# Softmax reciprocals as powers of minus one on GpSimd, in an attention and feed-forward kernel

## The chip, the cores and the metric

The kernel runs on one core of a Trainium2 chip. The core has five engines with an instruction queue each: TensorE (PE in the profile; its weight loads are listed apart as PEld), VectorE (DVE), ScalarE (ACT), GpSimd (POOL) and SyncE (SP), which here only issues transfers. An engine works through its queue strictly in order; semaphores make an instruction wait for one of another engine, or of its own. The metric is the device time of one execution in microseconds (us).

## What is computed

```
def _attn_ref(q, k, v):                      # (8, 8, 576, 64) each
    scores = scale * np.matmul(q, k.transpose(0, 1, 3, 2))
    kth = np.partition(scores, -32, axis=-1)[..., -32:-31]
    scores = np.where(scores >= kth, scores, -1000000000.0)
    scores = scores - np.max(scores, axis=-1, keepdims=True)
    attn = np.exp(scores)
    attn = attn / (np.sum(attn, axis=-1, keepdims=True) + 1e-09)
    return np.matmul(attn, v)

def _moe_ref(x, w_in, w_out):                # 4608 rows, 512 -> 2048 -> 512
    r = np.maximum(x @ w_in, 0.0)
    return (r * r) @ w_out
```

Attention over 8 batches of 8 heads keeps, for each query, only the 32 largest of its 576 scores. Its result, heads side by side, goes through a feed-forward layer with a squared relu.

## The kernel before

**Tiles.** Heads are taken in pairs (32 pairs), and the queries of a pair in blocks of 128 (four, and a rest of 64 that is joined with the rest of the next pair). That makes 144 groups; each group holds two heads' scores of 128 queries, 2 x 576 columns.

**One group.** PE makes the scores in PSUM, and ScalarE copies them to the tile `s` (L651). VectorE folds them with maxima into a tile `f` (L715, three folds). GpSimd does integer arithmetic on the same tiles (L710): two instructions write `u`, and one writes the low half of `f` from `u` and `f`; this last one is called "low" in this text. VectorE then finds the 32nd largest score by rounds of eight maxima and match-replace (L736, L741, L745, L748; result `kth`). ScalarE makes a mask `w` (L756), PE transposes scores and adds the mask (L476, L473), and ScalarE takes the exponential, `p` (L804). PE multiplies with V, to which a column of ones has been added, so that column 64 of each 65 holds the softmax sum.

**Where the change is.** This is the function `collect`: ScalarE copies the product from PSUM to `av` (L833), VectorE takes the reciprocals of column 64 into `rzall` (L835), GpSimd multiplies by them and writes `x` in bf16 (L837), and SP issues a transposing transfer of `x` into `xt` (L847, L850). `collect` is called 88 times: 56 times for two groups together (4 columns of `rzall`), 32 times for one (2 columns). `rzall` is read once more at the end, where `verdict` checks its largest and smallest element (L1027, L1028).

**The feed-forward part** (`feed`) takes `xt` in chunks: PE multiplies with the first weights, ScalarE applies the relu (L879), the square is taken by GpSimd (L893), ScalarE (L896) or, for the last two chunks, VectorE (L890); PE multiplies with the second weights, ScalarE copies (L913), and SP stores (L921).

**The order.** Nothing in the code says in which order an engine works. Each operation is entered with its engine, an assumed duration, a priority (lower goes first) and its dependencies; `late` delays the moment from which it may be taken. A planner (`Plan.schedule`) plays this through and, whenever an engine is free, takes the ready operation with the lowest priority. The five orders so found are emitted, with the semaphore waits that the dependencies need. Priorities are times: `tg` is a group's due time, `tt` the one at which its attention product is due. Buffers are given out in the same play; `f` has four, `u` one, `av` three, `x` four.

A second plan follows in the program, a full search that runs only when `verdict` raises a flag.

Of the kernel before, what the change touches and what calls it, by code (L numbers as in the profile page):

```python
# [5 lines left out]
ALU = mybir.AluOpType  # L6
# [6 lines left out]
P = 128  # L13
# [296 lines left out]
def bass_top_k_attn__then__act_relu_squared_kernel(  # L310
# [24 lines left out]
    def sb(name, shape, dt=FP32, n=None):  # L335
        if n is None:
            return nc.alloc_sbuf_tensor(name, shape, dt)
        return [nc.alloc_sbuf_tensor(f"{name}{i}", shape, dt) for i in range(n)]
# [27 lines left out]
    LATE = 2.3  # L366
# [14 lines left out]
    rzall = sb("rzall", [P, NALL])  # L381
    fcmp = sb("fcmp", [P, NALL])
    fone = sb("fone", [P, 4])
    heads = sb("heads", [P, 2])
    flag = sb("flag", [1, 1], I32)
    win = sb("win", [P, NCT, DFF], BF16)
# [27 lines left out]
    def tile(nm):  # L414
        return Tile(pools[nm])

    def at(t):
        return mem[t.pool.name][t.slot]

    def bank(t, i=0):  # L420
        return ps32[:, BASE[t.pool.name] + t.slot + i, :]
# [9 lines left out]
    act, vec, gp, pe = nc.scalar, nc.vector, nc.gpsimd, nc.tensor  # L431
# [40 lines left out]
    def mm(o, l, r, start, stop=True):  # L472
        return pe.matmul(o, l, r, start=start, stop=stop, skip_group_check=True)  # L473
# [6 lines left out]
    def build(full, weights, pl):  # L480
# [331 lines left out]
        def collect(gi, groups, parts, hp, tt):  # L812

            av, avs, xr = Tile(psum), tile("av"), tile("x")
            nu = 2 * len(groups)
            r0 = state["u"]
            state["u"] += nu

            def fav(j, pt, vbs):
                o, pq = bank(av), at(pt)  # L820
                for h in range(2):
                    for qs, vb in ((slice(0, 64), vbs[0]), (slice(64, 128), vbs[-1])) if gi == Z else ((slice(0, 128), vbs[h]),):
                        vv, ou = at(vb), o[qs, 65 * (2 * j + h):65 * (2 * j + h) + 65]
                        for kb in range(4):
                            mm(ou, pq[:, 4 * h + kb, qs], vv[:, 4 * h + kb, :], j == 0 and h == 0 and kb == 0)
                        ins = mm(ou, pq[:, 8, qs], vv[:, 8 + h, :], False)
                return ins

            pts = [pt for pt, _ in groups]
            vbu = sorted({v for _, vbs in groups for v in vbs}, key=lambda t: t.num)  # L830
            pl.op("pe", .05 + .16 * nu, tt + 2, lambda: [fav(j, pt, vbs) for j, (pt, vbs) in enumerate(groups)][-1],
                  r=pts + vbu, w=[av], take=[av, avs, xr])
            pl.op("act", .19 + 65 * nu / 1200, tt + 3, lambda: act.copy(  # L833
                at(avs)[:, 0:nu, :], bank(av)[:, 0:65 * nu].rearrange("p (u c) -> p u c", c=65)), r=[av], w=[avs])
            rz = pl.op("dve", .1, tt + 4, lambda: vec.reciprocal(rzall[:, r0:r0 + nu], at(avs)[:, 0:nu, 64]), r=[avs], late=LATE)  # L835
            rzs.append(rz)
            pl.op("gp", .13 + .11 * nu, tt + 4, lambda: gp.tensor_tensor(  # L837
                at(xr)[:, 0:nu, :], at(avs)[:, 0:nu, 0:64],
                rzall[:, r0:r0 + nu].unsqueeze(2).broadcast_to([P, nu, 64]), ALU.mult),
                r=[avs], w=[xr], after=[rz])  # L840

            xt, col, first = parts

            def turn():
                x = at(xr)
                if gi == Z:
                    return [nc.sync.dma_start_transpose(  # L847
                        at(xt)[:, hp + i, col:col + 64].unsqueeze(1),
                        x[64 * i:64 * i + 64, 0:2, :].rearrange("p h d -> p (h d)")) for i in range(2)]
                return [nc.sync.dma_start_transpose(  # L850
                    at(xt)[:, hp, col:col + 64 * nu].rearrange("p (i q) -> p i q", q=P),
                    x[:, 0:nu, :].rearrange("p h d -> p (h d)"))]

            nd = 2 if gi == Z else 1
            pl.op("sp", 2.0, tt + 5, turn, r=[xr], w=[xt], take=[xt] if first else [], ndma=nd, bw=.5 * nd,
                  sem=lambda o: f"x{xr.slot}")
# [80 lines left out]
        for b in range(NB):  # L937
# [3 lines left out]
            for hp, gi in seq:  # L941
# [8 lines left out]
                tt = tg + PER + 2 - TA - TL * max(0, 1 - (NGRP - state["n"]) / NL)  # L950
# [5 lines left out]
                r0, n_ = 128 * js[0], 128 * len(js) if gi != Z else 64  # L956
# [12 lines left out]
    def setup(pl):  # L969
        i0 = pl.op("gp", .2, -100, lambda: gp.memset(ident32[:, :], 0.0))  # L970
        i1 = pl.op("gp", .3, -99, lambda: gp.affine_select(
            ident32[:, :], ident32[:, :], [[-1, P]], ALU.not_equal, 1.0, base=0, channel_multiplier=1), after=[i0])
        i2 = pl.op("gp", .3, -98, lambda: gp.tensor_copy(ident_bf[:, :], ident32[:, :]), after=[i1])
        i3 = pl.op("gp", .5, -97, lambda: gp.tensor_scalar(
            neg_bf[:, :], ident32[:, :], -1.0, None, ALU.mult), after=[i1])
        i4 = pl.op("gp", .5, -97, lambda: gp.tensor_scalar(
            steep_bf[:, :], ident32[:, :], STEEP, None, ALU.mult), after=[i1])
        h0 = pl.op("gp", .1, -97, lambda: gp.memset(heads[:, :], 0.0))
        h1 = pl.op("gp", .1, -96.9, lambda: gp.memset(heads[0:64, 0:1], 1.0), after=[h0, i2, i3, i4])
        h2 = pl.op("gp", .1, -96.8, lambda: gp.memset(heads[64:128, 1:2], 1.0), after=[h1])  # L980
        pre = [i2, i3, i4]
        for t in mem["vb"]:
            pre.append(pl.op("gp", .2, -96.5, lambda t=t: gp.memset(t[:, 0:8, D:D + 1], 1.0), after=[h2]))
            pre.append(pl.op("gp", .2, -96.4, lambda t=t: gp.tensor_copy(t[:, 8:10, D], heads[:, :]), after=[h2]))
        zeros = [pl.op("gp", .3, -97.5, lambda t=t: gp.memset(t[:, 8:10, :], 0.0)) for t in mem["rv"]]
        pre.append(pl.op("gp", .1, -95, lambda: gp.memset(fone[:, 3:4], 1.0)))
        weights = []
        wi = moe_w_in.rearrange("(ct p) f -> p ct f", p=P)
        wo_ap = moe_w_out.rearrange("(fb p) o -> p fb o", p=P)
        for i in range(16):  # L990
            s = tile("ws")
            if i < 8:
                half, ct = divmod(i, NCT)
                src = wi[:, ct, 1024 * half:1024 * half + 1024]
                dst = win[:, ct, 1024 * half:1024 * half + 1024]
                view = lambda s: at(s)[:, :]
            else:
                fb = 2 * (i - 8)
                src = wo_ap[:, fb:fb + 2, :]
                dst = wo[:, fb:fb + 2, :]  # L1000
                view = lambda s: at(s)[:, :].rearrange("p (f o) -> p f o", f=2)
            pl.op("sp", 4.0, WD * i - 60, lambda s=s, src=src, view=view: [nc.sync.dma_start(view(s), src)],
                  w=[s], take=[s], ndma=1, sem=lambda o: f"ws{o.takes[0].slot}", nbf=WN + WP * i, bw=BW * 2.5)
            eng, fn = ("act", act.copy) if i % 4 < WA else ("gp", gp.tensor_copy)
            weights.append(pl.op(eng, 1.1, WC * i, lambda s=s, dst=dst, view=view, fn=fn: fn(dst, view(s)), r=[s]))

        times = [.22 * i for i in range(int(WARM / .22))]
        times += [WARM + WSTEP * i for i in range(int((WEND - WARM) / WSTEP))]
        for x in times:
            t = Tile(psum)  # L1010
            pl.op("pe", .22, 1e5, lambda t=t: mm(bank(t), ident_bf[:, :], ident_bf[:, :].unsqueeze(1).broadcast_to(
                [P, 4, P]), True), w=[t], take=[t], after=[i2], nbf=x)
        return [i1], pre, zeros, weights
# [22 lines left out]

    main = Plan()
    early, pre, zeros, weights = setup(main)
    n_pre = len(main.ops)
    kths, rzs = build(False, weights, main)  # L1040
# [84 lines left out]
```

## Time and profile before

| what | us |
|---|---|
| median of 3 runs | 816.22 (814.95 to 816.54) |
| profiled execution | 815.42 |
| its span | 813.6 |
| VectorE busy | 773.0 |
| ScalarE busy | 704.8 |
| GpSimd busy | 701.0 |
| PE busy | 712.3 |
| 88 reciprocals on VectorE, sum of their durations | 14.1 |
| 88 multiplications on GpSimd | 46.9 |

The span runs from the first instruction that the profile shows to the last, the profiled execution's time has what lies around it as well. Busy time counts overlapping instructions of an engine once, while the sum of a group's durations counts them in full. A group's row reads: line, engine, operation, written tile <- read tiles, shapes, count | busy us, mean ns of one | idle time of the engine just before them and who ended it. A row of the waits reads: who waited <- for whom: us in total, times, longest.

### The profile page before, as it was taken

How to read it: one execution, taken by the hardware profiler on the slowest of the kernel's cores; microseconds unless marked ns; L12 is line 12 of the kernel's file. 1: busy time of each engine (PE TensorE's matmuls, PEld its weight loads, DVE VectorE, ACT ScalarE, POOL GpSimd, SP SyncE). 2: the span in 40 equal slices, each digit the busy share in tenths (PEclk: the TensorE clock that was granted, in tenths of full speed). 3: DMA queues.
4: the chain of work that ended last, by engine and by line, in shares of the span. 5: the costliest groups of instructions: out<-in, count | busy, mean ns of one | idle time of the engine just before them, and what ended most of it. 6: DMA issues, size and time to landing. Idle time of an engine off the chain costs nothing.

```text
span 813.6 us, 27365 instructions
## 1 busy us (share of the span) xinstructions
PE 712.3 (88%) x10399; PEld 531.1 (65%) x10457; DVE 773.0 (95%) x3711; ACT 704.8 (87%) x1057; POOL 701.0 (86%) x645
## 2 busy tenths in 40 slices
PE   8886888988889989888888989898798989999995
PEld 3564666666676666766677666666667666676773
DVE  3899999999999999999999999999999999999991
ACT  3888989999898898988989899999989889998881
POOL 6798998899999898998889887998889978999940
PEclk9999999999999999999999999999999999999999
DMA  8557342031320232211430123302232020100111
GB/s 194 128 155 193 103 114 60 13 85 39 92 65 13 67 77 72 52 35 34 97 92 7 36 65 93 81 18 53 50 90 54 9 61 7 50 11 20 37 34 34
DMA packets 146205, 52.74 MB, mean 65 GB/s; under 512 B 138384, under 2 KB 138384, under 8 KB 146064
## 3 DMA queue, kind: packets, MB, share of 16 engines
q1 hardware_dynamic: 145392, 50.73, 25.1%
q8 instruction: 84, 1.38, 0.7%
q14 instruction: 57, 0.47, 0.2%
q10 hardware_dynamic: 672, 0.16, 0.1%
HBM read 36.70 MB, written 9.44 MB: 57 GB/s over the span
## 4 chain that ended last, share of the span: by engine, by line
DVE 61%; PE 18%; ACT 16%; issue 3%; POOL 1%; DMA 0%; SPq 0%; DVEq 0%; POOLq 0%
DVE f L745 17%; PE ps L473 15%; DVE f L715 15%; DVE c L741 13%; DVE f L736 8%; DVE kth L748 7%; ACT s L651 5%; ACT p L804 4%; ACT w L756 3%; PE ps L476 3%; ACT g L879 2%; ACT g L896 1%; ACT av L833 1%; DVE rzall L835 0%; POOL g L893 0%
## 5 line engine op out<-in xcount | busy, mean ns | idle before, releaser
L710 POOL TENSOR_TENSOR f<-u,f 128x864 int32<-128x864 int32 x144 | 269.6, 1872 | 6.4
L745 DVE MATCH_REPLACE8 f<-c,f 128x98 f32<-128x98 f32 (+2 forms) x864 | 228.1, 271 | 0.0
L756 ACT ACTIVATE w<-s,kth 128x576 bf16<-128x576 f32 x288 | 215.4, 783 | 7.4 <-DVE kth L748 6.9
L710 POOL TENSOR_TENSOR u<-f,s 128x576 int32<-128x576 int32 x144 | 188.2, 1307 | 30.9 <-DVE f L715 30.3
L473 PE MATMUL ps<-qk 64*128 64x192 f32 (+3 forms) x1280 | 192.1, 435 | 25.0 <-DVE f L715 24.1
L741 DVE MAX8 c<-f 128x8 f32<-128x98 f32 (+2 forms) x864 | 211.1, 275 | 0.0
L651 ACT COPY s<-ps 128x1152 f32<-128x1152 f32 x144 | 161.2, 1120 | 52.0 <-PE ps L473 51.2
L804 ACT ACTIVATE p<-ps 128x1152 bf16<-128x1152 f32 x144 | 163.3, 1134 | 18.1 <-PE ps L473 17.3
L473 PEld LDWEIGHTS ps<-qk 64*128 64x128 f32 (+1 forms) x1280 | 131.3, 177 | 65.2 <-DVE f L715 40.2
L473 PE MATMUL ps<-xt,win 128*128 128x256 bf16 (+1 forms) x1152 | 130.0, 266 | 14.4 <-ACT av L833 4.6
L710 POOL TENSOR_TENSOR u<-s 128x288 int32<-128x288 int32 x144 | 114.7, 796 | 30.5 <-ACT s L651 23.1
L476 PEld LDWEIGHTS ps<-ident,s 64*128 64x128 f32 x2592 | 107.9, 141 | 42.1 <-ACT w L756 28.8
L473 PE MATMUL ps<-wo,g 128*128 128x512 bf16 x518 | 122.8, 379 | 9.0 <-issue 5.1
L715 DVE TENSOR_TENSOR f<-ps,f 128x288 f32<-128x288 f32 x288 | 127.4, 442 | 0.2
L476 PE MATMUL ps<-ident,s 64*128 64x64 f32 x2592 | 110.5, 228 | 17.3 <-ACT w L756 17.2
L473 PEld LDWEIGHTS ps<-xt,win 128*128 128x128 bf16 x1152 | 98.5, 100 | 34.3 <-ACT g L879 6.5
L748 DVE MAX8 kth<-f 128x8 f32<-128x296 f32 x288 | 120.4, 457 | 0.0
L736 DVE MAX8 f<-f 128x8 f32<-128x288 f32 x288 | 119.0, 449 | 0.0
L879 ACT ACTIVATE g<-ps 128x512 bf16<-128x512 f32 x144 | 84.3, 604 | 10.0 <-PE ps L473 10.0
L473 PEld LDWEIGHTS ps<-wo,g 128*128 128x128 bf16 x576 | 51.4, 98 | 57.8 <-ACT av L833 1.3
L715 DVE TENSOR_TENSOR f<-ps,s 128x288 f32<-128x288 f32 x144 | 65.5, 455 | 16.7 <-ACT s L651 13.5
L473 PE MATMUL ps<-vb,p 128*128 128x65 bf16 (+1 forms) x1600 | 63.4, 197 | 13.6 <-ACT qk L602 4.2
(63 smaller groups left out, 741.4 us busy)
## 6 DMA issues: line engine op xcount, KB each, us to landing
rv<-in_v_dram SPq DMA_DIRECT2D x64, 128.0 KB, 2.5
out_dram<-o SPq DMA_DIRECT2D x32, 256.0 KB, 2.1
rk<-in_k_dram SPq DMA_DIRECT2D x63, 128.0 KB, 2.5
rq<-in_q_dram SPq DMA_DIRECT2D x62, 128.0 KB, 2.5
g<-in_moe_w_in_dram SPq DMA_DIRECT2D x8, 512.0 KB, 4.0
g<-in_moe_w_out_dram SPq DMA_DIRECT2D x8, 512.0 KB, 3.6
xt<-x SPq DMA_TRANSPOSE x72, 2.4
rq<-in_q_dram SPq DMA_DIRECT2D x32, 32.0 KB, 2.5
```

The source lines that it names most:

```text
L473: return pe.matmul(o, l, r, start=start, stop=stop, skip_group_check=True)
L476: return pe.matmul(o, i, ident, is_transpose=True, skip_group_check=True, **kw)
L651: cp = [pl.op("act", 1.2, tg - LEAD + 1, lambda: act.copy(at(st)[:, :, 0:S], two(banks(ss)[:, FIRST_AT:], SECOND, S)), r=[ss], w=[st])]
L710: return pl.op("gp", dur, prio, lambda: gp.tensor_tensor(o().bitcast(I32), x().bitcast(I32), y().bitcast(I32), op), **kw)
L715: return dve(.36, lambda: vec.tensor_tensor(o(), two(banks(ss)[:, FIRST_AT + c:], SECOND, QUART), x(), ALU.max), r=[ss], **kw)
L736: prev[i] = [dve(.065 + HALF / 960, lambda i=i: vec.max(at(f)[:, i, A + 7:A - 1:-1], at(f)[:, i, M + QUART:E]), after=prev[i] + [low], hol ...
L741: lambda i=i, t=t, c0=c0, c1=c1: vec.max(eighth(t, i), at(f)[:, i, c0:c1]),
L745: lambda i=i, t=t, c0=c0, c1=c1: vec.match_replace(at(f)[:, i, c0:c1], eighth(t, i), at(f)[:, i, c0:c1], NEG), hold=[f])]
L748: ks.append(chain(kth, i, prev[i], .065 + (8 + HALF) / 960, lambda i=i: vec.max(eighth(kth, i), at(f)[:, i, A:M + QUART]), hold=[f]))
L756: masks[i:] = [pl.op("act", .77, tw + .8 * i, lambda i=i: act.activation(at(wt)[:, i, :], at(st)[:, i, 0:S], ACTF.Relu, bias=kth[:, i, n:n ...
L804: return act.activation(at(pt)[:, :, :].rearrange("p c (h q) -> p h c q", h=2), bass.AP(x.tensor, x.offset, [x.ap[0], [APART, 2], [64, 9], ...
L879: return act.activation(at(g)[:, 0:kf * nt], bank(hh)[:, 0:kf * nt], ACTF.Relu)
```

## The change

The reciprocal is no longer taken by VectorE. GpSimd raises the sum to the power -1, with a constant tile `inv` of minus ones as the second operand, and its priority is 0.1 lower than that of the multiplication which follows. The assumed duration is the same 0.1 us; the delay `late=LATE` (2.3 us) is gone. The setup has one memset more, for `inv`.

```
@@ -832,7 +833,8 @@
             pl.op("act", .19 + 65 * nu / 1200, tt + 3, lambda: act.copy(
                 at(avs)[:, 0:nu, :], bank(av)[:, 0:65 * nu].rearrange("p (u c) -> p u c", c=65)), r=[av], w=[avs])
-            rz = pl.op("dve", .1, tt + 4, lambda: vec.reciprocal(rzall[:, r0:r0 + nu], at(avs)[:, 0:nu, 64]), r=[avs], late=LATE)
+            rz = pl.op("gp", .1, tt + 3.9, lambda: gp.tensor_tensor(
+                rzall[:, r0:r0 + nu], at(avs)[:, 0:nu, 64], inv[:, 0:nu], ALU.pow), r=[avs])
             rzs.append(rz)
@@ -976,9 +978,10 @@
         h0 = pl.op("gp", .1, -97, lambda: gp.memset(heads[:, :], 0.0))
-        h1 = pl.op("gp", .1, -96.9, lambda: gp.memset(heads[0:64, 0:1], 1.0), after=[h0, i2, i3, i4])
+        i5 = pl.op("gp", .1, -97, lambda: gp.memset(inv[:, :], -1.0))
+        h1 = pl.op("gp", .1, -96.9, lambda: gp.memset(heads[0:64, 0:1], 1.0), after=[h0, i2, i3, i4, i5])
-        pre = [i2, i3, i4]
+        pre = [i2, i3, i4, i5]
```

Both plans are built from the same functions, and the planner lays out all five engines' orders anew. In the new order each power waits for ScalarE's copy; between a power and its multiplication stands mostly one other instruction of GpSimd.

More of the change, by code (lines that the diff above doesn't have):

```diff
@@ L383, in bass_top_k_attn__then__act_relu_squared_kernel @@
     fone = sb("fone", [P, 4])
+    inv = sb("inv", [P, 4])
     heads = sb("heads", [P, 2])
```

## The prediction

> **What bounds the kernel now.** I read the page first (engine shares, chain), then who VectorE waited for, then busy time by stage, then the timeline around single reciprocals, and last the chain's final part.
>
> ```profile
> span 813.6 us, 27365 instructions
> PE 712.3 (88%) x10399; PEld 531.1 (65%) x10457; DVE 773.0 (95%) x3711; ACT 704.8 (87%) x1057; POOL 701.0 (86%) x645
> DVE 61%; PE 18%; ACT 16%; issue 3%; POOL 1%; DMA 0%; SPq 0%; DVEq 0%; POOLq 0%
> ```
>
> VectorE (DVE) is busy for 95% of the span and holds 61% of the chain that ended last. The profiled execution took 815.42 us as a whole, 1.8 us more than its span; the three timed runs have a median of 816.22, 0.8 us above it. I make the sum against 815.42.
>
> The next fence is all that VectorE waited for.
>
> ```profile
> DVE f L715 <- ACT s L651: 13.5, 13, 3.2
> DVE g L890 <- ACT g L879: 8.1, 4, 5.7
> DVE qk L530 <- PE ps L476: 6.6, 1, 6.6
> DVE rzall L835 <- ACT av L833: 0.8, 1, 0.8
> DVE flag L1035 <- PE ps L1033: 0.3, 1, 0.3
> ```
>
> No row names GpSimd (POOL): VectorE never waits for it, although every threshold search needs GpSimd's `f<-u,f` (below: "low"). The busy table by stage tells how near the two are (columns: stage, its length, then PE, PEld, DVE, ACT, POOL busy with instruction counts).
>
> ```profile
> 40.00:200.00 160.00, 135.56 (x2009) 101.82 (x2018) 157.53 (x761) 145.47 (x214) 148.45 (x132) 0.98 0.37 97
> 200.00:700.00 500.00, 443.64 (x6593) 335.12 (x6626) 494.47 (x2383) 451.78 (x682) 445.05 (x391) 0.98 0.23 55
> 700.00:760.00 60.00, 56.92 (x907) 44.27 (x913) 59.65 (x290) 53.81 (x81) 56.16 (x55) 1.00 0.10 29
> ```
>
> From 40 to 760 us VectorE idles 720 - (157.53 + 494.47 + 59.65) = 8.4 us: it alone sets the pace there. GpSimd's room is 11.6 us of 160, then 55 of 500, then 3.8 of 60. From about 757 us on the chain belongs to others:
>
> ```profile
> 756.86 0.97 POOL f L710
> ...
> 758.86 1.11 POOL x L837 x3
> 759.96 1.88 POOL g L893 x2
> 761.91 1.04 POOL g L893
> ...
> 765.00 3.25 PE ps L473 x23
> ```
>
> So what leaves VectorE before 757 us counts, what leaves it later does not, and work put on GpSimd between 757 and 765 us is on the chain itself.
>
> **What is removed: 88 reciprocals on VectorE.**
>
> ```profile
> L835 DVE RECIPROCAL rzall<-av 128x4 f32<-128x4 f32 x56 | 9.2, 165 | 0.0
> L835 DVE RECIPROCAL rzall<-av 128x2 f32<-128x2 f32 x32 | 4.9, 152 | 0.8 <-ACT av L833 0.8
> ```
>
> The rows give 9.2 + 4.9 = 14.1 us, but instructions of VectorE overlap, so I take what a reciprocal does to the start of the next one. First without a reciprocal between a match-replace and the next value load, then with one; then a maximum followed by a fold, with one at 398.77 between, and without.
>
> ```profile
> 406.53 0.26 DVE L745 MATCH_REPLACE8 f<-c,f 128x116 f32<-128x116 f32 x1
> 406.71 0.08 DVE L745 MATCH_VALUE_LOAD f<-c,f 128x8 f32 x1
> ...
> 411.86 0.27 DVE L745 MATCH_REPLACE8 f<-c,f 128x116 f32<-128x116 f32 x1
> 412.04 0.17 DVE L835 RECIPROCAL rzall<-av 128x4 f32<-128x4 f32 x1
> 412.13 0.06 DVE L745 MATCH_VALUE_LOAD f<-c,f 128x8 f32 x1
> ```
>
> ```profile
> 398.03 0.83 DVE L748 MAX8 kth<-f 128x8 f32<-128x296 f32 x2
> 398.77 0.16 DVE L835 RECIPROCAL rzall<-av 128x4 f32<-128x4 f32 x1
> 398.89 0.46 DVE L715 TENSOR_TENSOR f<-ps,s 128x288 f32<-128x288 f32 x1
> ...
> 419.48 0.83 DVE L748 MAX8 kth<-f 128x8 f32<-128x296 f32 x2
> 420.34 0.46 DVE L715 TENSOR_TENSOR f<-ps,s 128x288 f32<-128x288 f32 x1
> ```
>
> In the first place the step from replace to load grows from 0.18 to 0.27 us: the reciprocal costs 0.09. In the second the step is 0.86 us either way: it costs nothing. The timeline has 80 reciprocals from 38.08 to 759.11 us; by my count over it nine of them stand at places of the second kind, where the step does not change. I take 71 x 0.085 = **6.0 us off VectorE's path**, less than half of the 14.1 that its busy time suggests. The eight later ones lie where the chain has left VectorE: nothing.
>
> **What is added: 88 powers on GpSimd.** No row of this trace shows a power. The nearest rows are the multiplications beside which it is put (they wait on VectorE at times, and the last two rows here show the spacing of starts without a wait).
>
> ```profile
> L837 POOL TENSOR_TENSOR x<-av,rzall 128x256 bf16<-128x256 f32 x56 | 34.4, 614 | 7.0 <-DVE rzall L835 6.7
> L837 POOL TENSOR_TENSOR x<-av,rzall 128x128 bf16<-128x128 f32 x32 | 12.5, 396 | 13.8 <-DVE rzall L835 13.7
> L710 POOL TENSOR_TENSOR f<-u,f 128x864 int32<-128x864 int32 x144 | 269.6, 1872 | 6.4
> ...
> 399.54 0.62 POOL L837 TENSOR_TENSOR x<-av,rzall 128x256 bf16<-128x256 f32 x1
> 400.11 1.20 POOL L710 TENSOR_TENSOR u<-f,s 128x576 int32<-128x576 int32 x1
> ```
>
> A multiplication of 128x256 holds GpSimd for 400.11 - 399.54 = 0.57 us; three of 128x128 for 759.96 - 758.86 = 1.10, that is 0.37 each. The slope is 0.20 / 128 = 1.6 ns per column and the rest 0.17 us. A power of 4 columns at that rate would be 0.17 us, the lower bound. Above, a power is no single arithmetic step; 0.57 us would mean that four columns of it cost what 256 of the multiplication cost, and 1.87, the longest row of GpSimd, is the far end. I take **0.4 us**, nearer to 0.57 than to the floor, and keep 0.17 and 1.2 us for the range (1.2 is midway between 0.57 and 1.87).
>
> Where it lies: in the order of the new kernel every power waits for the copy on ScalarE (`av`, L833) and stands as soon as that copy is planned to end, without the delay of 2.3 us that the reciprocal had. What is queued behind it on GpSimd is u, low, the cast of V and the squares; VectorE waits for low, PE for the squares. Between power and multiplication there mostly stands one other GpSimd instruction, so its result is there in time. Against that, GpSimd loses its waits for VectorE's reciprocals, 20.4 us, of which the last four take 12.3 at the end, where nothing is behind them.
>
> What hides it is GpSimd's lead: how long a low ends before its group's first match-replace.
>
> ```profile
> 26.55 2.02 POOL L710 TENSOR_TENSOR f<-u,f 128x864 int32<-128x864 int32 x1
> 29.19 0.24 DVE L745 MATCH_REPLACE8 f<-c,f 128x98 f32<-128x98 f32 x1
> ...
> 221.34 1.71 POOL L710 TENSOR_TENSOR f<-u,f 128x864 int32<-128x864 int32 x1
> 235.45 0.25 DVE L745 MATCH_REPLACE8 f<-c,f 128x98 f32<-128x98 f32 x1
> ```
>
> These are groups 2 and 40: the lead is 0.6 us at the start and 12.4 us later. So the early stage decides. From 40 to 200 us there are 16 reciprocals, and with VectorE's 1.3 us less the room is 10.3 us: up to 0.64 us for each power, wait included, GpSimd keeps pace. From 200 to 700 (51 of them) the room is 50.9, 1.0 us each. From 700 to 760 (12) the room is 0.24 each, but there the lead covers 12 us. At 0.4 us all of it is hidden until 757.
>
> After 757 it is not: three or four powers come before the squares that PE waits for, 4 x 0.4 = **+1.6 us**. The last power, 0.4 in place of 0.17, is hidden: the multiplication ended at 795.3, and its transpose was issued only at 797.12.
>
> ```profile
> 794.95 0.40 POOL L837 TENSOR_TENSOR x<-av,rzall 128x128 bf16<-128x128 f32 x1 [1.90 <-DVE rzall L835]
> ...
> 797.12 1.11 SPq L850 DMA_TRANSPOSE xt<-x  x1
> ```
>
> The memset of `inv` goes into GpSimd's idle start before the first scores; if it were not hidden it would be 0.1 us.
>
> **What is moved: everything.** A planner orders all five engines, and taking 88 instructions from one and giving them to another changes its order from the first of them on; queues, transposes and loads move with it. The constants of the planner were chosen with the old order, and the new instruction is planned at 0.1 us. A new order can gain or lose; I bound it by -2 us (a quarter of VectorE's 8.4 us of idle time disappears) and +8.4 (it doubles), and take +1.
>
> Sum: 815.42 - 6.0 + 1.6 + 1.0 = **812.0 us**.
>
> **A rule on first calls.** The first use of another GpSimd operation shows no gap here: the affine select starts as early as 1.17 us and takes 0.29, and the new kernel has no further library instruction on that queue. The Trainium skill ("GPSIMD Engine Reference", Instruction dispatch) says that the first call to a freshly loaded kernel pays about 6 us of code load that no instruction shows. By it the sum would be about 817, since the first power comes near 38 us, where the lead is about 1 us. The trace so far shows nothing of that kind.
>
> ```profile
> 1.17 0.29 POOL L971 TENSOR_SCALAR_AFFINE_SELECT ident<-ident 128x128 f32<-128x128 f32 x1
> ```
>
> **Rivals.**
> (a) *GpSimd becomes the bound.* Place: the power itself and its wait for the copy, from 40 us on. It decides from 0.64 us each early, 1.0 later; with VectorE's 6 us gained it is slower than before from about 1.05. At 1.2 us: 16 x 0.56 = 9, 51 x 0.2 = 10, 12 x 0.96 = 11.5, 30 in all; 815.4 - 6 + 30 = **839 us**. For it: 86% busy already, little lead early, a power is the one operation without a row. Against: 1.2 us is seven times the multiplication's floor.
> (b) *The new order loses what VectorE gained.* VectorE's idle time doubles, +8.4, mostly by score copies that come later (its 13.5 us row): 815.4 - 6.0 + 1.6 + 8.4 = **819.4**. For it: the old order leaves VectorE 1.2% of idle time from 40 to 760, hard to match by one that nobody adjusted. Against: VectorE always has another group to work on.
> (c) *A stop at the first power* (the rule's effect). A stop of T us at 38 us gives 812 + T - 1; by the affine select's 0.29 us it is nothing, and T has to reach 4 to cancel the gain: about **815.4**.
> (d) *The change does not do what it says*: the freed slots are filled with waits that the reciprocals had hidden, as at 398.77 in all places: **815 to 816**.
>
> **How the numbers follow.** Forecast 0.42, (a) 0.26, (b) 0.22, (c) 0.04, (d) 0.06. A measurement of this kernel tells about 0.2% (1.6 us) from no change. Faster: the forecast and a little of (b), 0.43. Same: (d), part of (c), 0.09. Slower: (a) and most of (b), 0.48. The likeliest single case is 812, its own range 807 (floor price, order -2) to 815. Since the signs are near even, the range over all cases runs from 806 to 843, the upper end being (a) at 1.2 us with order +4; dearer powers are the part left out.
>
> **What would show it.** Right: VectorE busy about 767 (its rows for L835 gone, the other groups unchanged), no row of VectorE waiting for `f<-u,f`, powers spaced below 0.6 us, GpSimd's waits for the reciprocals gone, the chain on VectorE until about 750. Wrong: a power whose spacing exceeds 0.64 us and VectorE's match-replace waiting for GpSimd's low (a); VectorE's waits for the score copies well above 13.5 us (b); a gap before the first power alone (c); reciprocals gone with VectorE's steps unchanged (d).

## The result, and the profile after

| what | before, us | after, us |
|---|---|---|
| median of 6 runs each | 815.59 (813.0 to 816.54) | 827.41 (824.07 to 832.62) |
| profiled execution | 815.42 | 828.35 |
| its span | 813.6 | 826.3 |

The time after is 1.016 of the time before, with a 95% interval of 1.0139 to 1.0181: slower, by 11.8 us between the medians. The forecast was 812.0 us.

The page of the changed kernel, its busy times and the engines' shares of the chain that ended last:

```profile
PE 726.0 (88%) x10457; PEld 531.3 (64%) x10457; DVE 763.6 (92%) x3623; ACT 703.6 (85%) x1057; POOL 773.2 (94%) x734
DVE 50%; POOL 23%; PE 10%; ACT 7%; issue 6%; DMA 1%; SPq 1%; POOLq 0%; DVEq 0%
```

VectorE lost 9.4 us of work (773.0 to 763.6), and GpSimd gained 72.2 (701.0 to 773.2): it is now the busiest engine, and its share of the chain went from 1% to 23%. What a power costs stands in the groups kept apart by shape, and in the timeline, where the next start shows what an instruction really holds:

```profile
L836 POOL TENSOR_TENSOR rzall<-av,inv 128x4 f32<-128x4 f32 x56 | 56.6, 1010 | 2.4 <-ACT av L834 2.4
L836 POOL TENSOR_TENSOR rzall<-av,inv 128x2 f32<-128x2 f32 x32 | 22.6, 707 | 7.5 <-ACT av L834 7.5
```

```profile
344.61 1.01 POOL L836 TENSOR_TENSOR rzall<-av,inv 128x4 f32<-128x4 f32 x1
345.59 0.80 POOL L711 TENSOR_TENSOR u<-s 128x288 int32<-128x288 int32 x1
...
773.76 0.69 POOL L836 TENSOR_TENSOR rzall<-av,inv 128x2 f32<-128x2 f32 x1
774.43 1.04 POOL L895 TENSOR_TENSOR g<-g 128x512 bf16<-128x512 bf16 x1
```

Four columns hold GpSimd for 345.59 - 344.61 = 0.98 us, two for 774.43 - 773.76 = 0.67, so a column costs some 0.16 us on top of 0.35. Over the run that is 56 x 0.98 + 32 x 0.67 = 76 us. The room it had to fit into shows in the busy time by stage (columns as in the prediction, the fourth stage is new):

```profile
40.00:200.00 160.00, 136.19 (x2003) 101.33 (x2004) 155.71 (x741) 144.26 (x213) 157.02 (x144) 0.98 0.38 96
200.00:700.00 500.00, 446.53 (x6570) 331.78 (x6568) 482.75 (x2307) 446.18 (x677) 487.32 (x441) 0.98 0.23 55
700.00:760.00 60.00, 58.91 (x892) 42.94 (x884) 59.76 (x285) 54.91 (x79) 59.03 (x59) 1.00 0.10 26
760.00:795.00 35.00, 26.41 (x429) 20.16 (x429) 30.14 (x147) 23.55 (x39) 34.61 (x39) 0.96 0.09 25
```

From 40 to 760 us GpSimd's idle time is 16.6 us (70.3 before), VectorE's 21.8 (8.4 before): what VectorE no longer computes, it waits. For what, its waits say:

```profile
DVE f L716 <- ACT s L652: 27.4, 14, 8.3
DVE f L746 <- POOL f L711: 9.1, 5, 5.5
```

The waits for score copies have doubled (13.5 before), with one of 8.3 us among them, and the waits for GpSimd's low are new. GpSimd's lead of low over the match-replace, 2.6 to 4.9 us before in groups 16 to 24, is 0.2 to 1.3 there. One of these groups, its low and the first match-replace that needs it:

```profile
114.81 2.02 POOL L711 TENSOR_TENSOR f<-u,f 128x864 int32<-128x864 int32 x1
117.01 0.24 DVE L746 MATCH_REPLACE8 f<-c,f 128x98 f32<-128x98 f32 x1
```

The low ends at 116.83, which leaves 0.2 us. Later the lead recovers, mostly to 3 to 11 us (12 before), and is 0.2 again in the last three groups.

**Where the 12.7 us of span were lost.** Group for group, by the start of the first match-replace, the timelines of before and after can be laid beside each other. Here are groups 64, 72, 138 and 143 of after:

```profile
363.23 0.25 DVE L746 MATCH_REPLACE8 f<-c,f 128x98 f32<-128x98 f32 x1
...
414.69 0.25 DVE L746 MATCH_REPLACE8 f<-c,f 128x98 f32<-128x98 f32 x1
...
767.06 0.25 DVE L746 MATCH_REPLACE8 f<-c,f 128x98 f32<-128x98 f32 x1
...
798.56 0.09 DVE L746 MATCH_VALUE_LOAD f<-c,f 128x8 f32 x1 [5.48 <-POOL f L711]
798.64 0.25 DVE L746 MATCH_REPLACE8 f<-c,f 128x98 f32<-128x98 f32 x1
```

The same four groups stand at 362.89, 405.71, 761.53 and 784.76 before. The third kernel of the table is the first experiment, `e1_mult`: the changed kernel with every instruction where it was, but each power replaced by a multiplication by one (0.15 us), so that its output is not normalised.

| stretch | before, us | after, us | `e1_mult`, us | after less `e1_mult` |
|---|---|---|---|---|
| start to group 64 | 362.9 | 363.2 | 359.9 | 3.4 |
| group 64 to 72 | 42.8 | 51.5 | 43.1 | 8.4 |
| group 72 to 138 | 355.8 | 352.4 | 348.4 | 4.0 |
| group 138 to 143 | 23.2 | 31.6 | 23.3 | 8.3 |
| group 143 to the end | 28.8 | 27.7 | 25.6 | 2.1 |
| span | 813.6 | 826.3 | 800.2 | 26.1 |

Two short stretches, eight groups and five, hold 16.7 of the 26.1 us. Nearly all of it is VectorE's waiting: its waits add up to 53.1 us in after and to 27.5 in `e1_mult`. Up to group 138 the score copies make most of the difference (25.9 us against 13.6) and low little (2.3 against none); behind it low has 6.8.

**The stall at 362 us.** The timeline of after, one collect from its copy to the feed that needs it (brackets: idle time of the engine before the instruction, and who ended it):

```profile
360.77 0.38 ACT L834 COPY av<-ps 128x260 f32<-128x260 f32 x1
...
366.63 1.01 POOL L836 TENSOR_TENSOR rzall<-av,inv 128x4 f32<-128x4 f32 x1
367.71 0.61 POOL L839 TENSOR_TENSOR x<-av,rzall 128x256 bf16<-128x256 f32 x1
368.35 1.20 SPq L852 DMA_TRANSPOSE xt<-x  x1
371.79 1.87 PE L474 MATMUL ps<-xt,win 128*128 128x256 bf16 x8 [6.12 <-issue]
...
375.55 2.29 PE L474 MATMUL ps<-qk 64*128 64x192 f32 x8
...
377.89 1.12 ACT L652 COPY s<-ps 128x1152 f32<-128x1152 f32 x1 [1.18 <-PE ps L474]
379.04 0.46 DVE L716 TENSOR_TENSOR f<-ps,s 128x288 f32<-128x288 f32 x1 [8.33 <-ACT s L652]
```

The same collect in `e1_mult`:

```profile
357.39 0.38 ACT L834 COPY av<-ps 128x260 f32<-128x260 f32 x1
358.33 0.20 POOL L836 TENSOR_TENSOR rzall<-av,inv 128x4 f32<-128x4 f32 x1
358.61 0.61 POOL L839 TENSOR_TENSOR x<-av,rzall 128x256 bf16<-128x256 f32 x1
359.25 1.20 SPq L852 DMA_TRANSPOSE xt<-x  x1
362.12 1.04 PE L474 MATMUL ps<-xt,win 128*128 128x256 bf16 x8
```

The order is the same in both, and the copy is done at 361.15 in the one and 357.77 in the other. In `e1_mult` GpSimd comes to this place 0.56 us after the copy, in after 5.48 us: it runs late (its timeline has no gap of more than 0.2 us from 353 to 368 us), and the power waits in the queue, not for data. The multiplication, the transpose and `xt` are late by these 4.9 us more, and by another 0.8 that the power takes longer. PE's queue has the first matmul of the feed ahead of the next scores, so PE stands for 6.12 us. (The profile names "issue" there, which is no releaser; that it is the transpose is read from the times: its data landed 3.3 us after it was issued, and the matmul starts 3.4 us after.) The next scores come at 375.55, their copy at 377.89, and VectorE waits 8.33 us for it: the longest of the waits that doubled.

**The end.** The chain of waits of after, from group 138 on (start, us, engine, tile, line):

```profile
763.08 1.96 POOL u L711 x2
...
766.83 0.71 POOL rzall L836 x2
...
768.86 0.66 POOL rzall L836
...
773.80 0.65 POOL rzall L836
...
779.56 0.65 POOL rzall L836
...
784.61 0.66 POOL rzall L836
...
790.80 0.65 POOL rzall L836
...
792.52 3.72 PE ps L474 x18
...
809.01 0.71 POOL rzall L836
```

From 763 to 792.5 us the chain runs on GpSimd, and seven powers lie on it (the first row of `rzall` has two; by their starts each holds 0.66 us); the one at 809 is the last collect's. Before, GpSimd's part of the chain ended with PE's matmuls at 765 us.

### The profile page after: what moved, and what is told of

It is laid out like the page before. It is cut to its first block, busy times and chain, and to the rows that moved or that the text cites. A ratio compares the mean times of both kernels' runs of the same rounds, so it can differ in the third digit from the quotient of the medians.

```text
span 826.3 us, 27388 instructions
## 1 busy us (share of the span) xinstructions
PE 726.0 (88%) x10457; PEld 531.3 (64%) x10457; DVE 763.6 (92%) x3623; ACT 703.6 (85%) x1057; POOL 773.2 (94%) x734
## 4 chain that ended last, share of the span: by engine, by line
DVE 50%; POOL 23%; PE 10%; ACT 7%; issue 6%; DMA 1%; SPq 1%; POOLq 0%; DVEq 0%
DVE f L746 15%; DVE f L716 12%; DVE c L742 11%; POOL u L711 9%; PE ps L474 9%; POOL f L711 9%; DVE f L737 7%; DVE kth L749 5%; POOL rzall L836 2%; ACT s L652 2%; ACT p L805 2%; ACT w L757 1%; POOL g L895 1%; PE ps L477 1%; POOL x L839 1%
## 5 line engine op out<-in xcount | busy, mean ns | idle before, releaser
L746 DVE MATCH_REPLACE8 f<-c,f 128x98 f32<-128x98 f32 (+2 forms) x864 | 225.8, 267 | 0.0
L742 DVE MAX8 c<-f 128x8 f32<-128x98 f32 (+2 forms) x864 | 206.7, 270 | 0.0
L474 PE MATMUL ps<-xt,win 128*128 128x256 bf16 (+1 forms) x1152 | 131.8, 267 | 24.8 <-DMA xt<-x 6.7
L474 PE MATMUL ps<-wo,g 128*128 128x512 bf16 x576 | 139.6, 383 | 10.2 <-POOL g L895 7.7
L836 POOL TENSOR_TENSOR rzall<-av,inv 128x4 f32<-128x4 f32 (+1 forms) x88 | 79.2, 900 | 9.9 <-ACT av L834 9.9
```

The costliest lines, as they stand in the source:

```text
L742: lambda i=i, t=t, c0=c0, c1=c1: vec.max(eighth(t, i), at(f)[:, i, c0:c1]),
L746: lambda i=i, t=t, c0=c0, c1=c1: vec.match_replace(at(f)[:, i, c0:c1], eighth(t, i), at(f)[:, i, c0:c1], NEG), hold=[f])]
L836: rz = pl.op("gp", .1, tt + 3.9, lambda: gp.tensor_tensor(rzall[:, r0:r0 + nu], at(avs)[:, 0:nu, 64], inv[:, 0:nu], ALU.pow), r=[avs])
```

## The experiments

Each was timed against the kernel before on the same chip; intervals are 95%. Of several on one question the edits stand together.

**1. What do the powers cost, in the new order and in the old?** `e1_mult`, against after; `e2_extra`, against before, keeps the reciprocals and adds 88 powers whose results nobody uses.

```
 e1_mult
-    rzall[:, r0:r0 + nu], at(avs)[:, 0:nu, 64], inv[:, 0:nu], ALU.pow), r=[avs])
+    rzall[:, r0:r0 + nu], at(avs)[:, 0:nu, 64], inv[:, 0:nu], ALU.mult), r=[avs])
...
 e2_extra
+ def scaled():
+     gp.tensor_tensor(spare[:, r0:r0 + nu], at(avs)[:, 0:nu, 64], inv[:, 0:nu], ALU.pow)
+     return gp.tensor_tensor(at(xr)[...], at(avs)[:, 0:nu, 0:64], rzall[...], ALU.mult)
```

> The changed kernel with its five orders unchanged, but the 88 powers are multiplications by one of the same shape, so that rzall holds the sums and the output is not normalised. Theory D (duration: a power of 0.98 us for 4 columns and 0.66 for 2 makes the multiplication's result, and with it the transposes that TensorE waits for, late, and fills GpSimd in the last groups): without the long duration the loss goes and VectorE's 6 us are gained, 807 to 812 us, no wait of 8 us at 379 us, GpSimd's small operation spaced 0.2 us. Theory O (order: the new order itself is worse than the old one): stays at 820 to 828.

> The kernel before with its orders unchanged and the reciprocals still on VectorE; GpSimd computes 88 powers as well, each right ahead of its multiplication, into a tile that nobody reads. Theory D: GpSimd gets 79 us more, its lead over VectorE shrinks to a few us, the last groups are bound by GpSimd: 819 to 828. Theory O: the old order bears it, 815 to 818.

Measured: `e1_mult` 802.59 us, 0.9842 of before (0.9821 to 0.9864), faster than either reading allowed; `e2_extra` 838.41, 1.0286 (1.0262 to 1.031), slower than either. The powers cost 827.4 - 802.6 = 24.8 us in the new order and 838.4 - 814.7 = 23.7 in the old. So it is the work on GpSimd and not where the planner put it; and with a cheap operation there, the new order and VectorE's shorter work beat before by 12 us.

**2. Is it the planned duration?** The planner took a power for 0.1 us. `e3_planned` tells it the truth.

```
-            rz = pl.op("gp", .1, tt + 3.9, ...
+            rz = pl.op("gp", .34 + .16 * nu, tt + 3.9, ...
```

> The changed kernel with the power's duration told to the planner as measured (0.34 us and 0.16 per column in place of 0.1), so a new order. Theory D: TensorE's stalls for late transposes go (some 10 us), but GpSimd is still 94% busy and bounds the last groups: 814 to 821. Theory O in its form that only the wrong planned duration is to blame: 812 or less. If any new order is bad: above 822.

Measured: 860.78 us, 1.0564 (1.0531 to 1.0597), 33 us slower than after. Two waits that grew by 19 us and more beside after, in its waits:

```profile
POOL rzall L836 <- ACT av L834: 40.0, 25, 5.4
DVE f L746 <- POOL f L711: 28.1, 25, 3.0
```

GpSimd now stands for ScalarE's copy for 40.0 us (9.9 in after): in this order the power comes too early in a queue that cannot let others pass. Why the planner with a truer number lays out a worse order, the runs do not settle (see 7).

**3. Is it the delay that went with the reciprocal?** `e4_nolate`, before without `late=LATE`.

```
-            rz = pl.op("dve", .1, tt + 4, ..., r=[avs], late=LATE)
+            rz = pl.op("dve", .1, tt + 4, ..., r=[avs])
```

> The kernel before, reciprocals on VectorE, only without the delay of 2.3 us that the change removed as well; again a new order. Theory D: the delay and the order matter little, 813 to 819. Theory O: a new order without adjusted constants costs as much as the change did, 820 to 828.

Measured: 816.85 us, 1.0026 (1.0005 to 1.0047). It is neither the loss nor the gain.

**4. What were the reciprocals worth?** `e5_double` takes each reciprocal of before twice. `e11_back` gives 88 reciprocals back to VectorE in `e1_mult`, one ahead of the last maximum of eleven in eighteen searches.

```
 e5_double
+            lambda: [vec.reciprocal(t[:, r0:r0 + nu], at(avs)[:, 0:nu, 64]) for t in (spare, rzall)][-1]
...
 e11_back
+            if i == 0 and n % 18 < 11: vec.reciprocal(spare[:, 4 * n:4 * n + 4], inv[:, :])
```

> The kernel before with its orders unchanged, but VectorE takes each reciprocal twice, the first into a tile that nobody reads. It measures what a reciprocal costs on VectorE. Sizing S (0.085 us each up to 757 us, as the steps in the timeline gave): 5 to 7 us slower, 820 to 822. Sizing B (VectorE's busy time fell by 9.8 us with the multiplications in place of the powers, so 0.12 or more each): 9 to 13 us slower, 824 to 828.

> The kernel with multiplications by one in place of the powers and the changed kernel's orders (802.6 us), to which 88 reciprocals of 4 columns are added on VectorE, one ahead of the last maximum of 88 groups, written to a tile that nobody reads; the output is not normalised. If a reciprocal's 0.06 to 0.09 us add up in this order too: 807 to 810, and what is left to the 814 of the kernel before, some 5 us, is the order and no longer waiting for VectorE. If the whole 12 us were the reciprocals' own: 812 or more. If VectorE does not bound this order: 802 to 804.

Measured: `e5_double` 819.72, 1.0069 (1.0048 to 1.009), 5.5 us above before; `e11_back` 806.38, 0.9894 (0.9865 to 0.9923), 3.8 above `e1_mult`. What a reciprocal costs is again far below its row: 5.5 us for 88 are 0.06 us each. `e11_back` has as many instructions on VectorE as before (3711) and is still 8.0 us faster. This rest belongs to the new order, with the normalisation no longer passing through VectorE; it is a difference of runs. Part of it can be read in the traces. From 30 us to group 138 VectorE is busy for 723.2 of 731.5 us before, and in `e11_back`, with as many instructions, for 719.6 of 725.0: 3.6 us less work and 2.9 less idle time. The shorter work fits a count: in that stretch a group's first fold that directly follows a maximum of L748 starts 0.49 us after it, any other instruction 0.38. Before has 80 such folds there, the new order 54, which makes 26 x 0.11 = 2.9 us.

**5. From which price does a power cost time, and where?** `e6_half` puts an idle multiplication of 130 columns ahead of each multiplication of `e1_mult`. `e7_late` has powers only in the last 18 collects, `e8_early` only in the first 70.

```
 e6_half
+ gp.tensor_tensor(spare[:, r0 // 2 % 8, :], at(avs)[:, 0:2, :].rearrange("p u c -> p (u c)")[:, 0:W], wide[:, 0:W], ALU.mult)
...
 e7_late
+ o_ = ALU.pow if r0 >= 252 else ALU.mult
...
 e8_early
+ o_ = ALU.pow if r0 < 252 else ALU.mult
```

> The changed kernel's orders, the powers replaced by multiplications by one as before, and ahead of each a multiplication of 128x130 into a tile that nobody reads, so that some 0.5 us stand on GpSimd where the power took 0.98 or 0.66; the output is not normalised. Threshold reading (up to 0.64 us each are hidden by GpSimd's lead, as the prediction had it): 803 to 806. Proportional reading (each 0.1 us costs what it costs, whatever the lead): 802.6 + 24.8 x 0.35 / 0.72 = 814, within 4.

> The changed kernel's orders, with powers only in the last batch (the last 18 of 88) and multiplications by one in the others; part of the output is not normalised. If the last groups are bound by GpSimd, the 18 powers cost nearly their full extra time, 18 x 0.51 = 9 us: 809 to 812. If the loss is all in the middle: 802 to 804.

> The other way round: powers in the first 70, multiplications by one in the last batch; part of the output is not normalised. If the loss splits between the middle (late transposes, TensorE stalled) and the end (GpSimd bound): 814 to 819, and the two parts add up to the 25 us between all powers and none. If the end alone: 803 to 806.

Measured: `e6_half` 809.97, 0.9945 (0.9928 to 0.9962); `e7_late` 810.29, 0.9963 (0.9941 to 0.9984); `e8_early` 816.69, 1.0029 (1.0004 to 1.0054). Of `e6_half`, a pair of starts in the timeline gives the price of what was added:

```profile
352.96 0.46 POOL L840 TENSOR_TENSOR spare<-av,wide 128x130 bf16<-128x130 f32 x1
353.38 0.20 POOL L841 TENSOR_TENSOR rzall<-av,inv 128x4 f32<-128x4 f32 x1
```

0.42 us in 88 places cost 7.4 us (810.0 - 802.6). Where, the first match-replaces of groups 138 and 143 of `e6_half` tell:

```profile
750.83 0.25 DVE L749 MATCH_REPLACE8 f<-c,f 128x98 f32<-128x98 f32 x1
...
778.59 0.09 DVE L749 MATCH_VALUE_LOAD f<-c,f 128x8 f32 x1 [4.75 <-POOL f L714]
778.67 0.25 DVE L749 MATCH_REPLACE8 f<-c,f 128x98 f32<-128x98 f32 x1
```

In `e1_mult` group 138 stands at 751.33: up to there the added work cost nothing, as the prediction's threshold has it. The two profiled spans differ by 6.3 us (806.5 and 800.2; this execution of `e6_half`, 808.40 us, is the fastest of its ten), and all of that lies behind: 27.8 us against 23.3 from group 138 to 143, and 27.8 against 25.6 from there to the end. The powers, 0.71 us more than a multiplication on average (76 us less 88 x 0.15, over 88), lost 15.8 us up to group 138 as well.

The first 70 powers cost 14.1 us, the last 18 cost 7.7, together 21.8 of 24.8 (both kernels raise to the power 1, which takes 0.98 and 0.66 us as well). By stretches, `e8_early` loses 13.7 us ahead of group 138 and nothing behind it, `e7_late` 0.8 ahead and 6.8 behind; all powers together lose 15.8 and 10.4, more in each part than the two do apart.

**6. Is it GpSimd's room?** If so, taking other work off GpSimd returns the loss, and does less for before. `SQ` sets how many of eight squares GpSimd takes; the others go to ScalarE. `e9_sq2` and `e9_sq1` are after with 2 and 1 for 3, `e12_before_sq1` is before with 1.

```
-    SQ = 3
+    SQ = 1
```

> The changed kernel with 2 instead of 3 of 8 squares on GpSimd and the others on ScalarE, outside the last batch: GpSimd gets some 13 instructions of 1.0 us less, ScalarE as many of 0.64 more; a new order. If GpSimd's load is what costs: 4 to 12 us faster than the changed kernel, 815 to 823. If the orders' accidents decide: anywhere from 815 to 845.

> The same with 1 of 8 squares on GpSimd, some 30 us less for it and 19 more for ScalarE, which is 85% busy. If GpSimd's load is what costs: 808 to 818, at best as fast as the kernel before. If the end, where all squares stay on GpSimd, decides: 815 to 822. If ScalarE becomes the bound: above 825.

> The kernel before, reciprocals on VectorE, with 1 of 8 squares on GpSimd; a new order. It is the control for the changed kernel with 1 of 8 squares (809.0 us). If VectorE is the bound of the kernel before, relieving GpSimd gives nothing: 811 to 819. If the 809 came from moving the squares alone: 806 to 810.

Measured: `e9_sq2` 822.77, 1.0102 (1.0068 to 1.0136); `e9_sq1` 808.98, 0.9931 (0.9911 to 0.9951); `e12_before_sq1` 810.11, 0.9951 (0.9931 to 0.9972). The same setting is worth 18.4 us to after and 3.4 to before. The step from 3 to 2 brings 4.6 and that from 2 to 1 brings 13.8; whether a limit is passed there or the new orders do it, the runs do not tell.

The last batch still took its squares on GpSimd, where `e9_sq1` had VectorE waiting 5.6 us for low. `e13_last` drops that exception in `e9_sq1`, `e14_before_last` in `e12_before_sq1`.

```
-                elif last or i * SQ % 8 < SQ:
+                elif i * SQ % 8 < SQ:
```

> The changed kernel with 1 of 8 squares on GpSimd in the last batch too, where before all were (outside the last two chunks). If GpSimd's load bounds the last groups: the 8 to 10 us lost there come back for the most part, 799 to 804. If the loss there has another cause, such as the wait for the attention product: 807 to 811.

> The same two settings in the kernel before, with the reciprocals on VectorE (control; without the setting for the last batch it took 810.1). GpSimd was not the bound of its last groups: 807 to 812. If the change is worth VectorE's 5.5 us once GpSimd has room, the changed kernel is some 5 us faster than this one.

Measured: `e13_last` 802.81, 0.986 (0.9821 to 0.9899); `e14_before_last` 808.05, 0.9925 (0.9902 to 0.9949). The page of `e13_last`, and the first of its waits of VectorE:

```profile
PE 717.0 (89%) x10457; PEld 519.7 (65%) x10457; DVE 759.3 (95%) x3623; ACT 721.0 (90%) x1097; POOL 735.2 (92%) x694
```

```profile
DVE f L716 <- ACT s L652: 16.0, 8, 3.5
```

VectorE is back at 95%, GpSimd below it, VectorE has no wait for low at all, and the longest wait for a score copy is 3.5 us in place of 8.3. Groups 64 to 72 take 41.5 us and groups 138 to 143 24.0: both losses are gone. `e13_last` computes the reference in full, with the powers, and beats before by 1.4%, and after by 3%. Beside its control, which has an order of its own, the change is then worth 808.05 - 802.81 = 5.2 us.

**7. Once more the planned duration, with room.** `e15_planned_sq1` is `e9_sq1` with `.34 + .16 * nu`.

> The changed kernel with 1 of 8 squares on GpSimd (last batch as before) and the power's measured duration told to the planner. If the harm of the true duration came from a plan in which GpSimd is nearly full: 806 to 815. If a true duration is bad as such: 830 or more.

Measured: 828.5 us, 1.0193 (1.0144 to 1.0242), 19.5 above `e9_sq1`, between what the two readings allowed. One row of its waits:

```profile
POOL rzall L836 <- ACT av L834: 39.0, 35, 5.8
```

GpSimd's wait for the copy is as long as in `e3_planned`, though GpSimd has more room, but the harm is less than the 33 us there. So GpSimd's load is at most a part of what makes the truer number harmful; what the rest is in the planner's play stays open.

## Why the prediction was wrong

**The reciprocals, -6.0 us: right.** 5.5 us by doubling them in the old order, 3.8 by giving them back in the new one, and not the 14.1 of their rows. VectorE's busy time fell to 763.6, even below the 767 foreseen, since its other instructions too follow one another more closely in the new order (experiment 4).

**The power, 0.4 us: wrong, and this is the first step that failed.** It costs 0.98 and 0.67 us. Both lie inside the bounds of 0.17 and 1.2, but above the 0.64 us up to which the prediction itself lets GpSimd keep pace early; the value was taken near the multiplication's row, and a multiplication of the same four columns costs 0.15.

**"At 0.4 us all of it is hidden until 757": borne out at that price.** With 0.42 us added, `e6_half` reaches group 138 as early as `e1_mult`. At the real price 15.8 us are lost up to there, and mostly not by the way that the prediction watched. It read the cover off one consumer, VectorE with its lead of low. The powers lie on a second way as well: copy, power, multiplication, transpose, `xt`, PE's feed, and behind the feed in PE's queue the next scores, which VectorE needs too. Low's lead of some 2 us at 362 us hid nothing when GpSimd reached the power 5.5 us after the copy; PE stood 6.1 us, VectorE 8.3.

**+1.6 after 757: wrong, the second step that failed.** It is not the price alone: with 0.42 us added, the stretches behind group 138 already lose 4.5 + 2.2 = 6.7 us, and with the powers 8.3 + 2.1 = 10.4. The prediction left GpSimd's part of the chain where it was, ending at 765 us with three or four powers on it. In the new order it lasts to 792.5, with seven powers of about 0.7 us. The lead that the sum relied on ends there: before, it was 13 us at group 140 but 3.7 at group 143; after, 0.2.

**+1 for the new order: wrong in sign.** By `e11_back` the new order is worth 8.0 us, beyond the bound of -2. So the result is 814.4 - 8.0 (order) - 3.8 (reciprocals in that order) + 24.8 (powers) = 827.4; these are differences between neighbouring runs, so the sum closes by itself. At the assumed 0.4 us the kernel would lie, by estimate, between `e1_mult` (0.15 us, 802.6) and `e6_half` (0.15 + 0.42, 810.0), so the sign would have held. The sum's 812 would still have been too high: the gain of order that it lacks is larger than the loss at the end that it put too low.

**The rivals.** (a), GpSimd as the bound, comes nearest, at 0.98 us rather than 1.2, but its sign, VectorE waiting for low, shows mainly at the end (6.8 of 9.1 us); up to group 138 a late GpSimd reached VectorE through the score copies. Its arithmetic at the measured price, 16 x (0.98 - 0.64) + 12 x (0.66 - 0.24) = 10.5 us, plus four powers of 0.66 at the end and the order's +1, gives 815.4 - 6 + 10.5 + 2.6 + 1 = 823.5, against 828.35: right in sign, 5 us short. With the order's -8 in place of +1 it would be 14 short: it counts room only, and not the stall and the end. Its "slower than before from about 1.05" does not follow from its own terms: with the last 12 collects, which its 839 us count, 16 x (p - 0.64) + 12 x (p - 0.24) uses up the 6 us gained at p = 0.68. (b) fell: VectorE's waits for score copies did double, its sign in the profile, but with the same order and a cheap operation (`e1_mult`) they are 13.6 us, as before. The late power made them, not the order. (d) fell with `e5_double`. (c) fell with the first power:

```profile
36.97 1.04 POOL L836 TENSOR_TENSOR rzall<-av,inv 128x4 f32<-128x4 f32 x1
37.99 1.71 POOL L711 TENSOR_TENSOR f<-u,f 128x864 int32<-128x864 int32 x1
```

It takes what all others take, and the next instruction starts 1.02 us after it. The code load of about 6 us that the Trainium skill ("GPSIMD Engine Reference", Instruction dispatch) describes for the first call to a freshly loaded kernel is not to be seen at this operation.

## What to carry to other kernels

Price an operation that the trace doesn't show by its operation and not by its size: here four columns of a power cost more than 256 columns of a multiplication (0.98 and 0.57 us), and the upper bound deserved the weight. Before calling work on an engine hidden, list every consumer of what is queued behind it and the lead of each, transfers and in-order queues behind them included; the shortest lead counts, and it changes over the run: here 0.42 us more per collect was hidden for 750 us and not behind. Work moved onto an engine that is 86% busy may need other work moved off it first: with most squares given to ScalarE, the same change turns from +1.6% into -0.65% against its control.

## What the hardware showed beside

TensorE's granted clock halved after one long idle time. The stretch of the stall in after, in steps of 4 us (last three columns: granted clock, DMA share, GB/s; from 362 to 366 us the clock is 1.00):

```profile
366.00:370.00 4.00, 0.00 (x0) 0.00 (x0) 4.00 (x21) 0.60 (x1) 3.78 (x5) 0.88 0.13 28
370.00:374.00 4.00, 1.87 (x8) 1.05 (x8) 0.71 (x3) 0.31 (x1) 3.86 (x3) 0.50 0.19 68
374.00:378.00 4.00, 3.66 (x36) 3.39 (x38) 0.00 (x0) 2.60 (x6) 3.06 (x4) 0.50 0.02 4
378.00:382.00 4.00, 3.64 (x53) 2.98 (x50) 2.96 (x13) 3.70 (x7) 3.92 (x5) 0.84 0.43 97
```

The 0.88 and 0.84 of the outer rows put the ends of the half rate near 369.0 and 379.3 us: it begins some 3.4 us into the 6.1 us without a matmul and lasts some 10 us. The eight matmuls of the feed take 1.87 us, 1.04 in `e1_mult`, and the scores behind them 2.29, 1.24 there: one late transfer is paid twice, once as idle time and once as slower matmuls behind it. The Trainium skill ("TensorE: Matmul & The Clock Gate", Part 1, the HAM clock gate) states half rate after an idle window of about 3.4 us and full rate after about as long a busy one. The trace agrees on the half rate; the clock came back to full only some 7.5 us after the first matmul at 371.79, with another gap of 0.7 us among them.
